# Attention and feed-forward on one core: the half-made words of the weight conversions in an idle PSUM bank

## The chip, the cores and the metric

The kernel runs on one core of one Trainium2 chip. Its time is the device time of one execution in microseconds (us); the figure before the change is the median of three runs. The profile is one execution recorded by the hardware profiler on the same core. Engines: PE is TensorE's matmul, PEld its weight load, DVE VectorE, ACT ScalarE, POOL GpSimd, SP the engine whose queue issues the DMAs.

## The reference

Attention in which a query sees only the keys of its own hash bucket, and then a feed-forward layer on the result:

```
q, k, v: (4, 8, 768, 64)      proj: (64, 6)
bucket(x) = sum over 6 bits of 2^i * (x @ proj > 0)
scores = q @ k^T / 8,  -1e9 where bucket(q) != bucket(k)
attn = exp(scores - rowmax);  attn /= sum(attn) + 1e-9
x = (attn @ v), heads side by side: (3072, 512)
h = x @ w_in (512 x 2048)
g = h if h >= 1;  0 if h <= -1;  (h + 1)^2 / 4 between
out = g @ w_out (2048 x 512)
```

The weights come as 64-bit floats. The matmuls run on rounded 32-bit numbers (fp32r); for accuracy an operand is split into a rounded high part and the low rest, and three products are added (high by high, high by low, low by high).

## The kernel before

**Heads and units.** The 32 heads (hd) are worked one after the other, two to a pair. A head has 12 units: two halves (hf) of 384 queries by six blocks (j) of 128 keys. The loop at line 609 runs over all units g, and its order is the order on every engine; the schedule is written by hand. In each turn the program issues, in this order: the score products of unit g (`s_unit`, L371 and L372) and ACT's two exponentials (L380 rounded, L385 plain); the DVE reduction of the last maximum product (`max_red`, L314), if the turn before issued one; the subtraction that makes the low part of unit g-1 (`lo_unit`, L39, on DVE, but on POOL for j = 0 and 3); the three value products of unit g-4 (`pv_unit`, L404 to L406); in every even unit two maximum products for the head after next (`max_mm`, L310); and last the tasks that are listed for that unit (`at(g, ...)`). "Unit 9" below means the turn for unit 9 of a head.

**PSUM.** There are eight banks: four score tiles in a ring (`ps_s`), two output banks (`obank`), and a two-bank tile for the maximum products (`ps_m`, tile smax, one buffer). `obank[0]` collects the value products of the first half, in units 4 to 9 of the head, and ACT copies it out (L412) behind unit 9; it then lies idle until unit 4 of the next head. `obank[1]` collects the second half, from unit 10 to unit 3 of the next head.

**Hash and maximum.** For each pair the hash products (`bits_mm`, L210: four matmuls for each half) go into an idle output bank; ACT copies the negated low rows out (L216), DVE compares (`bits_cmp`, L221), POOL scales (`bits_scale`, L273), SP puts the result in its place. Their operands are made by POOL in units 0 to 3 (`cast_h` L152, `low_h` L39, one pair of them per unit, all queued behind `max_clamp` L342). The negated row maxima of a head are clamped, transposed on PE (`max_tr`, L349) into a PSUM bank at unit 4, and copied by ACT at unit 5 (`max_put`, L354).

**Weight conversions.** `WeightSplit.steps` turns a 64-bit block (128 x 512) into a 32-bit float by integer operations: s0 loads the raw words (`wraw`), s1 squares the high word on ACT (L69) and starts the word `wa` on DVE (L70), s2 (L74) and s3 (L78) put in sign and low bits, s4 (L82) multiplies by a flag into `wsq`, s5 and s6 make the high and low parts (ACT L87, POOL L39), `put` stores. Heads 3 to 26 each begin one such conversion: twelve of w_in in the odd heads, twelve that are parked in DRAM in the even ones. `conv` lists the steps by units counted from the head's first: 0 for s0, 7 for s1, 9 for s2, 13 (unit 1 of the next head) for s3, 15 for s4. The word lives in an SBUF tile with one buffer.

**Feed-forward.** Behind the attention come the two layers (`gemm1` and the product loop, L959 and L1054 for the first, L822 for the second). Eight blocks of w_out are converted there, with POOL unused.

Of the kernel before, what the change touches and what calls it, by code (L numbers as in the profile page):

```python
# [11 lines left out]
F32 = mybir.dt.float32  # L12
F32R = mybir.dt.float32r
I32 = mybir.dt.int32
# [8 lines left out]
P = 128  # L23
# [4 lines left out]
DM = H * D  # L28
# [9 lines left out]
def sub(nc, eng, out, a, b):  # L38
    eng.tensor_tensor(out=out, in0=a, in1=b, op=ALU.subtract)  # L39


class WeightSplit:
# [7 lines left out]
        nc.vector.memset(sc[:, 1:2], 29)  # L50
        self.sc = sc

    def steps(self, src, shape, hi, lo, cp, stage=None, low=None, keep=None):
        nc, n = self.nc, self.n
        st = {}

        def s0():
            st["raw"] = self.pool.tile([P, n, 2], I32, name="wraw")
            dst = st["raw"]
            if len(shape) == 4:  # L60
                dst = dst.rearrange("p (c f) t -> p c f t", c=shape[1])
            nc.sync.dma_start(out=dst, in_=src)

        def s1():
            raw = st["raw"]
            sq = st["sq"] = self.pool.tile([P, n], F32, name="wsq")
            a = st["a"] = self.pool.tile([P, n], I32, name="wa", bufs=1)
            high = raw[:, :, 1].bitcast(F32)
            nc.scalar.activation(out=sq, in_=high, func=AF.Square)  # L69
            nc.vector.tensor_scalar(out=a, in0=raw[:, :, 1], scalar1=0x07FFFFFF, scalar2=3,  # L70
                                    op0=ALU.bitwise_and, op1=ALU.logical_shift_left)

        def s2():
            nc.vector.scalar_tensor_tensor(out=st["a"], in0=st["raw"][:, :, 1], scalar=self.sc[:, 0:1],  # L74
                                           in1=st["a"], op0=ALU.bitwise_and, op1=ALU.bitwise_or)

        def s3():
            nc.vector.scalar_tensor_tensor(out=st["a"], in0=st["raw"][:, :, 0], scalar=self.sc[:, 1:2],  # L78
                                           in1=st["a"], op0=ALU.logical_shift_right, op1=ALU.bitwise_or)

        def s4():
            nc.vector.scalar_tensor_tensor(out=st["sq"], in0=st["sq"], scalar=WMIN2,  # L82
                                           in1=st["a"].bitcast(F32), op0=ALU.is_ge, op1=ALU.mult)

        def s5():
            if cp is nc.scalar:
                cp.copy(out=hi, in_=st["sq"])  # L87
            else:
                cp.tensor_copy(out=hi, in_=st["sq"])

        def s6():
            sub(nc, low or nc.gpsimd, lo, st["sq"], hi.bitcast(F32))

        def put():
            nc.sync.dma_start(out=keep if stage is None else stage, in_=st["sq"])

        if stage is None:
            return [s0, s1, s2, s3, s4, s5, s6] + ([put] if keep is not None else [])

        def get(sq=None):  # L100
            st["sq"] = self.pool.tile([P, n], F32, name="wsq") if sq is None else sq
            nc.sync.dma_start(out=st["sq"], in_=stage)

        return [s0, s1, s2, s3, s4, put], [get, s5, s6]


# [4 lines left out]
NU = 2 * NJ  # L111


def attention(ctx, tc, wst, T1, T2, qk, v, pj, cv, x_d, s_d, e_d, tasks, shared):
    nc = tc.nc
    const = ctx.enter_context(tc.tile_pool(name="aconst", bufs=1))
    work = ctx.enter_context(tc.tile_pool(name="awork", bufs=2))
    small = ctx.enter_context(tc.tile_pool(name="asmall", bufs=2))
    shared["work"], shared["small"] = work, small
    ps_s = ctx.enter_context(tc.tile_pool(name="ps_s", bufs=4, space=PSUM))  # L120
    ps_o = ctx.enter_context(tc.tile_pool(name="ps_o", bufs=1, space=PSUM))
    ps_m = ctx.enter_context(tc.tile_pool(name="ps_m", bufs=1, space=PSUM))
    obank = [ps_o.tile([P, 512], F32, name=f"o{i}") for i in range(2)]
# [193 lines left out]
    mx = {}  # L317
# [26 lines left out]
        eng.tensor_scalar(out=nm[:, 0:NJ], in0=nm[:, 0:NJ], scalar1=CLAMP, scalar2=None,  # L344
                          op0=ALU.min)

    def max_tr(hd, bank):
        ps = mx[hd] = obank[bank]
        nc.tensor.transpose(out=ps[0:2 * NJ, 0:P], in_=nms.pop(hd), identity=ident)  # L349

    def max_put(hd):
# [98 lines left out]
    def raw0():  # L450
        return wst.tile([P, DM, 2], I32, name="wraw").rearrange("p a b -> p (a b)").bitcast(F32)[:, 0:S].rearrange(
            "p (h s) -> p h s", h=1)

    def at(g, fn, *a):
        tasks[g].append((fn, a))

    first = [raw0(), raw0()]
# [92 lines left out]
    at(12, bits_put, 1)  # L550
    at(12, move, 1, 2)
    at(12, max_tr, 0, 0)
    at(12, max_put, 0)
    at(10, load_raw, 2)
# [4 lines left out]
    at(15, row_flags, 1)  # L559
    at(12, lambda: nc.gpsimd.memset(T2[2][0:64, 0].bitcast(F32), 0.0))  # L560
    at(17, max_tr, 1, 1)
    at(17, max_put, 1)
    at(18, half_clamp, 2, 0)
# [4 lines left out]
    for hd in range(NH):  # L568
        pr, h = hd // 2, hd % 2
        g = hd * NU  # L570
        if 0 < hd < NH - 2:
            gc, gt = ((g + NU + 6, g + NU + 7) if hd == 1 else (g + NU + 2, g + NU + 4) if hd == 2
                      else (g + NU, g + NU + 4))
            at(gc, max_clamp, hd + 2, nc.gpsimd if hd > 2 else nc.vector)
            at(gt, max_tr, hd + 2, 1)
            at(gt + (hd > 1), max_put, hd + 2)
        if h == 0 and pr + 2 < NPAIR:
            g0 = g + (13, 2)[pr] if pr < 2 else g
            for n in range(4):
                at(g0 + n, cast_h, pr + 2, nc.gpsimd, n % 2, n // 2)  # L580
                at(g0 + n, low_h, pr + 2, nc.gpsimd, n % 2, n // 2)
            at(g0 + 3, move, pr + 2, 0)
            at(g0 + 3, move, pr + 2, 1)
            at(g0 + 6, move, pr + 2, 2)
            if pr + 3 < NPAIR:
                at(g0 + 7, load_raw, pr + 3)
            bits_at = ((20, 1), (23, 0)) if pr == 0 else ((8 if pr == 1 else 7, 1), (11, 0))
            for hf, (n, bank) in enumerate(bits_at):
                at(g + n, bits_mm, pr + 2, hf, bank)
                at(g + n + 1, bits_cmp, pr + 2, hf)  # L590
            at(g + n + 1, move, pr + 2, 3)
            at(g + n + (2 if pr else 1), bits_scale, pr + 2, nc.gpsimd if pr else nc.scalar)
            at(g + (18 if pr else 25), bits_put, pr + 2)
        if h == 0 and pr + 1 < NPAIR:
            gv = g + LAG + (2 if pr else 16)
            at(gv, cast_v, pr + 1, nc.scalar)
            at(gv + 1, split_v, pr + 1, nc.gpsimd, 0)
            at(gv + 3, split_v, pr + 1, nc.gpsimd, 1)
            if pr + 2 < NPAIR:
                at(gv + (6 if pr else 4), load_v, pr + 2)  # L600
# [8 lines left out]
    for g in range(NG + LAG + 1):  # L609
# [7 lines left out]
        if g < 4 * NU:  # L617
            due = g in early
            hd, i = early.get(g, (0, 0))
        else:  # L620
            hd, i = g // NU + 2, g % NU // 2
# [18 lines left out]
NCT = DM // P  # L640
# [458 lines left out]
def lsh_attn_ffn(ctx: ExitStack, tc: tile.TileContext, qk, v, pj, cv, w_in, w_out, out):  # L1099
    nc = tc.nc  # L1100
# [13 lines left out]
    wq = [xdp.tile([P, DM], F32, name=f"wq{i}") for i in range(NFT)]  # L1114
# [16 lines left out]
    wih, wil = ([w[:, t] for w in wpair] for t in range(2))  # L1131
# [3 lines left out]
    win_v = w_in.bitcast(I32).rearrange("(ct p) (f t) -> p ct f t", p=P, t=2)  # L1135
    wout_v = w_out.bitcast(I32).rearrange("(ft p) (n t) -> ft p n t", p=P, t=2)
    wst = ctx.enter_context(tc.tile_pool(name="wst", bufs=2))
    ws = WeightSplit(nc, wst, DM)
# [4 lines left out]
    def at(g, fn, *a):  # L1143
        tasks[g].append((fn, a))

    def conv(g, steps, offs):
        for fn, n in zip(steps, offs):
            at(g + n, fn)

    def wi_steps(i, cp, stage=None):  # L1150
        return ws.steps(win_v[:, :, i * P:(i + 1) * P, :], (P, NCT, P, 2), wih[i], wil[i], cp, stage, None, wq[i])

    def wo_steps(i, cp, stage=None, low=None):
        return ws.steps(wout_v[i], (P, DM, 2), woh[i], wol[i], cp, stage, low)

    woh = [hi for hi, lo in wo]
    wol = [lo for hi, lo in wo]
    for i in range(NW1):
        conv((2 * i + 3) * NU, wi_steps(i, nc.scalar), (0, 7, 9, 13, 15, 17, 19, 21))
    g0 = (NH - 4) * NU  # L1160
    late = {}
    for n in range(NSTG):
        i = n - (NFT - NW1)
        stage = wq[NW1 + n] if i < 0 else xdp.tile([P, DM], F32, name=f"wd{n}")
        if i < 0:
            first, late[n] = wi_steps(NW1 + n, nc.vector, stage)
        elif i < 2:
            first, late[n] = wo_steps(i, nc.vector, stage)
        else:
            first, late[n] = wo_steps(i, nc.scalar, stage, nc.gpsimd if i < 4 else nc.vector)  # L1170
        conv((4 + 2 * n) * NU, first, (0, 7, 9, 13, 15, 16))
    for n, g in enumerate((1, 7, 13, 25, 30, 35)):
        conv(g0 + g, late[n], (0, 5, 6))

    actx = ExitStack()
    attn = {}
    for b in range(B - 1):
        g = (b + 1) * H * NU + LAG + 4
        at(g, lambda b=b: xm.sums_load(*(attn["small"].tile([P, NF], F32, name=n, bufs=1) for n in ("sm", "em")), b))
# [21 lines left out]
    for i in (2, 3):  # L1201
        at(NH * NU + 2 * i - 10, late[i + NFT - NW1][0])
    attention(actx, tc, wst, T1, T2, qk, v, pj, cv, x_d, s_d, e_d, tasks, attn)
    actx.close()

# [5 lines left out]
    for i in range(2, NFT):  # L1211
        n = i + NFT - NW1
        need = i + GLAG if i < LEAD else 2 * i + GLAG + 1 - LEAD
        if n < NSTG:
            get, cast, low = late[n]
# [68 lines left out]
```

## Time and profile before

| | |
|---|---|
| time, median of three runs | 981.41 us (980.84 to 982.14) |
| span of the profiled execution, first to last instruction | 980.2 us |
| PE busy in the span | 966.7 us |
| DVE busy | 793.9 us |
| ACT busy | 679.6 us |
| POOL busy | 346.3 us |
| attention | up to about 463.6 us |
| granted TensorE clock | 1.000 |

The profiled execution's own time is known as its span; the runs' times stand 1.2 us above it (981.41 against 980.2), for what lies around the first and last instruction. A profile line of the timeline has the start, the length, the engine, the line of the code, the operation and the tiles (out<-in). A line of instruction groups has the count behind an x, the busy time, the mean length in ns, and then the idle time of that engine just before them. A line of waits has who waited for whom, the total in us, how often, and the longest. The lines by stretches have the length, then busy time and count of PE, PEld, DVE, ACT and POOL, the granted clock, the DMA share and GB/s.

### The profile page before, as it was taken

Reading aid. Unit: us, or ns where it says so; the run is one execution under the profiler, and the core shown is the slowest. Engines: PE = TensorE matmul, PEld = TensorE weight load, DVE = VectorE, ACT = ScalarE, POOL = GpSimd, SP = SyncE. Lnnn points to the kernel's source line nnn. Section 1 sums busy time; section 2 is a strip of 40 time slices with the busy share of each in tenths; the row PEclk is TensorE's granted clock in tenths of the full one; section 3 lists DMA queues with packets and bytes.
Section 4 is the critical chain, followed back from the end, with each engine's and each line's share of the span. In section 5 each row is a group of like instructions: output and inputs, shape, how many; then the busy total and the mean of one; then the engine's idle time right before and its main releaser. Section 6 shows DMA issues by size and latency. Waiting matters only on the chain.

```text
span 980.2 us, 15590 instructions
## 1 busy us (share of the span) xinstructions
PE 966.7 (99%) x5050; PEld 889.7 (91%) x5050; DVE 793.9 (81%) x1359; ACT 679.6 (69%) x1481; POOL 346.3 (35%) x418
## 2 busy tenths in 40 slices
PE   8999999999999999999999999999999999999998
PEld 7889999999999999999999998888988889988886
DVE  8779999999999999887898887877866777655554
ACT  7878988898899898888655555455564545544444
POOL 8767777778887777666000000000000000000000
PEclk9999999999999999999999999999999999999999
DMA  6674667676666667644395478966458554454431
GB/s 164 178 189 108 165 175 184 192 180 192 168 159 162 177 174 187 161 119 126 126 319 185 129 237 287 314 223 205 116 157 240 149 183 119 143 159 119 117 88 65
DMA packets 95113, 167.56 MB, mean 171 GB/s; under 512 B 13956, under 2 KB 51960, under 8 KB 95032
## 3 DMA queue, kind: packets, MB, share of 16 engines
q1 hardware_dynamic: 94808, 166.56, 59.6%
q8 instruction: 40, 0.66, 0.3%
q14 instruction: 41, 0.34, 0.1%
q10 hardware_dynamic: 224, 0.00, 0.0%
HBM read 106.13 MB, written 33.87 MB: 143 GB/s over the span
## 4 chain that ended last, share of the span: by engine, by line
PE 87%; DVE 5%; ACT 3%; DMA 2%; issue 1%; POOL 1%; SPq 1%; DVEq 0%; ACTq 0%; POOLq 0%
PE y L822 27%; PE h L1054 18%; PE smax L310 7%; PE h L959 7%; PE o L406 5%; PE o L404 5%; PE o L405 5%; PE s L371 5%; PE s L372 5%; DVE nm L314 2%; PE o L210 2%; DVE pl L39 1%; DMA wraw<-in_w_in_dram 1%; ACT ph L380 1%; DMA sm<-sd 0%
## 5 line engine op out<-in xcount | busy, mean ns | idle before, releaser
L380 ACT ACTIVATE ph<-s 128x384 fp32r<-128x384 f32 x380 | 188.3, 496 | 41.1 <-PE s L372 35.1
L314 DVE TENSOR_REDUCE nm<-smax 128x1 f32<-128x768 f32 x189 | 179.0, 947 | 15.2 <-PE smax L310 13.6
L39 POOL TENSOR_TENSOR pl<-pf,ph 128x384 fp32r<-128x384 f32 x128 | 141.9, 1112 | 87.8 <-ACT pf L385 83.1
L787 DVE SCALAR_TENSOR_TENSOR t<-t 128x384 f32<-128x384 f32 x128 | 71.3, 557 | 101.6 <-ACT z L782 101.3
L39 DVE TENSOR_TENSOR pl<-s,ph 128x384 fp32r<-128x384 f32 x256 | 135.8, 544 | 10.8 <-ACT s L385 9.6
L371 PE MATMUL s<-t 128*128 128x384 f32 x384 | 132.2, 344 | 0.0
L404 PE MATMUL o<-ph,va 128*128 128x386 f32 x384 | 130.1, 339 | 1.1 <-DVE neg L221 1.1
L406 PE MATMUL o<-pl,va 128*128 128x386 f32 x384 | 130.1, 339 | 0.4 <-DVE pl L39 0.4
L405 PE MATMUL o<-ph,vb 128*128 128x386 f32 x384 | 130.1, 339 | 0.0
L372 PE MATMUL s<-t 128*128 128x384 f32 x384 | 129.3, 337 | 0.0
L385 ACT ACTIVATE s<-s 128x384 f32<-128x384 f32 x252 | 125.2, 497 | 0.0
L822 PE MATMUL y<-t,ghi 128*128 128x512 f32 x384 | 124.7, 395 | 0.0
L310 PE MATMUL smax<-t 128*128 128x384 f32 x378 | 103.1, 354 | 5.7 <-DVE nm L314 4.4
L781 ACT ACTIVATE t<-h,mh 128x384 f32<-128x384 f32 x56 | 32.6, 581 | 84.0 <-PE h L959 44.3
L310 PEld LDWEIGHTS smax<-t 128*128 128x128 f32 x378 | 64.4, 188 | 23.8 <-DVE nm L314 22.1
L792 ACT CAST ghi<-z 128x384 fp32r<-128x384 f32 x129 | 65.1, 505 | 30.1 <-DVE z L788 26.3
L782 ACT ACTIVATE z<-t,m 128x384 f32<-128x384 f32 x128 | 79.0, 617 | 4.2
L1054 PE MATMUL h<-wbig,t 128*128 128x384 f32 x399 | 81.4, 336 | 0.0
L822 PEld LDWEIGHTS y<-t,ghi 128*128 128x128 f32 x384 | 71.3, 188 | 11.1 <-ACT ghi L792 0.3
L1054 PEld LDWEIGHTS h<-wbig,t 128*128 128x128 f32 x399 | 71.6, 188 | 5.3
L781 ACT ACTIVATE t<-wsq,mh 128x384 f32<-128x384 f32 x48 | 29.6, 617 | 67.0 <-DVE wsq L1067 40.8
L822 PE MATMUL y<-t,glo 128*128 128x512 f32 x192 | 76.0, 396 | 0.0
(189 smaller groups left out, 2134.9 us busy)
## 6 DMA issues: line engine op xcount, KB each, us to landing
t<-wc SPq DMA_DIRECT2D x92, 256.0 KB
t<-t SPq DMA_DIRECT2D x60, 384.0 KB
wraw<-wc SPq DMA_DIRECT2D x76, 256.0 KB
raw<-in_qk_dram SPq DMA_DIRECT2D x14, 768.0 KB
wraw<-in_w_in_dram SPq DMA_DIRECT2D x16, 512.0 KB
wraw<-in_w_out_dram SPq DMA_DIRECT2D x16, 512.0 KB
t<-ed SPq DMA_DIRECT2D x36, 192.0 KB
xd<-xs SPq DMA_DIRECT2D x32, 192.5 KB
```

Of the source, the lines that this page charges most:

```text
L39: eng.tensor_tensor(out=out, in0=a, in1=b, op=ALU.subtract)
L310: nc.tensor.matmul(out=smax[hd][:, hf, 0:HS], lhsT=t2[:, 0, h, i * P:(i + 1) * P], rhs=t2[:, 1, h, hf * HS:(hf + 1) * HS], start=True, sto ...
L314: nc.vector.tensor_reduce(out=nmp(hd)[:, i:i + 1], in_=smax[hd][:, :, 0:HS], axis=AX.XY, op=ALU.max, negate=True)
L371: nc.tensor.matmul(out=ps[:, 0:HS], lhsT=t1[:, 1, h, ks], rhs=t1[:, 0, h, sl], start=True, stop=False)
L372: nc.tensor.matmul(out=ps[:, 0:HS], lhsT=t2[:, 1, h, ks], rhs=t2[:, 0, h, sl], start=False, stop=True)
L380: nc.scalar.activation(out=ph[:, 0:HS], in_=ps[:, 0:HS], func=AF.Exp, scale=SCALE)
L385: nc.scalar.activation(out=pf, in_=ps[:, 0:HS], func=AF.Exp, scale=SCALE)
L404: nc.tensor.matmul(out=o, lhsT=wa, rhs=ph, start=(jj == 0), stop=False)
L405: nc.tensor.matmul(out=o, lhsT=wb, rhs=ph, start=False, stop=False)
L406: nc.tensor.matmul(out=o, lhsT=wa, rhs=pl, start=False, stop=(jj == NJ - 1))
L822: nc.tensor.matmul(out=ys[c][m], lhsT=g_[:, m * P:(m + 1) * P], rhs=w, start=(first and k == 0), stop=(last and k == 2))
L1054: nc.tensor.matmul(out=ps, lhsT=w[:, cs], rhs=x, start=(n == 0 and s not in (2, 3, 6)), stop=(n == 5), skip_group_check=True)
```

## The change

The word of the conversions moves from SBUF into `obank[0]`, for the 24 conversions in the attention (those in the feed-forward part keep the SBUF tile). As that bank is idle only from unit 10 to unit 3 of the next head, the steps move: s1 and s2 both to unit 10, s3 to 12 (unit 0 of the next head), s4 to 14 (unit 2), s5, s6 and `put` one unit earlier. The hash products of a pair, from the fourth pair on, go one after the other into `obank[1]`, at units 5 and 7 in place of 7 (bank 1) and 11 (bank 0); the comparison, SP's last move and POOL's scale step follow them, at units 6 and 8, 8, and 9. The transposed maxima, which had lain in `obank[1]` at unit 4, take a tile of the score ring, from the sixth head's maxima on.

```diff
-    def steps(self, src, shape, hi, lo, cp, stage=None, low=None, keep=None):
+    def steps(self, src, shape, hi, lo, cp, stage=None, low=None, keep=None, word=None):
...
-            a = st["a"] = self.pool.tile([P, n], I32, name="wa", bufs=1)
+            a = st["a"] = self.pool.tile([P, n], I32, name="wa", bufs=1) if word is None else word()
...
-    shared["work"], shared["small"] = work, small
+    shared["work"], shared["small"], shared["word"] = work, small, lambda: obank[0].bitcast(I32)
...
-    def max_tr(hd, bank):
-        ps = mx[hd] = obank[bank]
+    def max_tr(hd, bank=None):
+        ps = mx[hd] = ps_s.tile([P, 512], F32, name="s") if bank is None else obank[bank]
...
-            at(gt, max_tr, hd + 2, 1)
+            at(gt, max_tr, hd + 2, 1 if hd < 3 else None)
...
-            bits_at = ((20, 1), (23, 0)) if pr == 0 else ((8 if pr == 1 else 7, 1), (11, 0))
+            bits_at = (((20, 1), (23, 0)), ((8, 1), (11, 0)))[pr] if pr < 2 else ((5, 1), (7, 1))
...
-        return ws.steps(win_v[:, :, i * P:(i + 1) * P, :], (P, NCT, P, 2), wih[i], wil[i], cp, stage, None, wq[i])
+        return ws.steps(win_v[:, :, i * P:(i + 1) * P, :], (P, NCT, P, 2), wih[i], wil[i], cp, stage, None, wq[i], word)
...
-        return ws.steps(wout_v[i], (P, DM, 2), woh[i], wol[i], cp, stage, low)
+        return ws.steps(wout_v[i], (P, DM, 2), woh[i], wol[i], cp, stage, low, None, None if stage is None else word)
...
-        conv((2 * i + 3) * NU, wi_steps(i, nc.scalar), (0, 7, 9, 13, 15, 17, 19, 21))
+        conv((2 * i + 3) * NU, wi_steps(i, nc.scalar), (0, 10, 10, 12, 14, 16, 18, 20))
...
-        conv((4 + 2 * n) * NU, first, (0, 7, 9, 13, 15, 16))
+        conv((4 + 2 * n) * NU, first, (0, 10, 10, 12, 14, 15))
```

More of the change, by code (lines that the diff above doesn't have):

```diff
@@ L1148, in conv, with word @@
             at(g + n, fn)
+    attn = {}
+    def word():
+        return attn["word"]()
     def wi_steps(i, cp, stage=None):
-        return ws.steps(win_v[:, :, i * P:(i + 1) * P, :], (P, NCT, P, 2), wih[i], wil[i], cp, stage, None, wq[i])
+        return ws.steps(win_v[:, :, i * P:(i + 1) * P, :], (P, NCT, P, 2), wih[i], wil[i], cp, stage, None, wq[i], word)
     def wo_steps(i, cp, stage=None, low=None):
-        return ws.steps(wout_v[i], (P, DM, 2), woh[i], wol[i], cp, stage, low)
+        return ws.steps(wout_v[i], (P, DM, 2), woh[i], wol[i], cp, stage, low, None, None if stage is None else word)
     woh = [hi for hi, lo in wo]
@@ L1175, in lsh_attn_ffn @@
     actx = ExitStack()
-    attn = {}
     for b in range(B - 1):
```

## The prediction

> **What bounds the kernel now.** I read the page's first part, then busy time by stretches, then the waits of the stretch that holds the edits, then single heads in the timelines.
>
> ```profile
> span 980.2 us, 15590 instructions
> PE 966.7 (99%) x5050; PEld 889.7 (91%) x5050; DVE 793.9 (81%) x1359; ACT 679.6 (69%) x1481; POOL 346.3 (35%) x418
> ...
> PE 87%; DVE 5%; ACT 3%; DMA 2%; issue 1%; POOL 1%; SPq 1%; DVEq 0%; ACTq 0%; POOLq 0%
> ```
>
> PE has work nearly all the time and makes 87% of the chain that ended last. The edits take no matmul away, so they can only win or lose what PE waits. Head 4 begins at 79.8 us and head 28 at 412.9; the feed-forward part begins at about 463.6.
>
> ```profile
> 79.80:412.90 333.10, 332.24 (x1850) 318.19 (x1849) 315.15 (x465) 300.38 (x720) 255.60 (x288) 1.00 0.65 172
> ...
> 463.60:980.20 516.60, 512.38 (x2546) 459.59 (x2544) 371.32 (x718) 273.93 (x517) 2.55 (x2) 1.00 0.57 175
> ```
>
> The columns after the length are PE, PEld, DVE, ACT and POOL. In those 24 heads DVE is busy 315.15 of 333.10 us, 95%. Busy PE hides short waits, because a matmul's record covers its pipeline, so I count starts instead.
>
> ```profile
> 271.75 0.33 PE L371 MATMUL s<-t 128*128 128x384 f32 x1
> ...
> 272.62 0.33 PE L371 MATMUL s<-t 128*128 128x384 f32 x1
> ...
> 273.85 0.33 PE L371 MATMUL s<-t 128*128 128x384 f32 x1
> ...
> 275.60 0.52 PE L310 MATMUL smax<-t 128*128 128x384 f32 x2
> 275.96 0.33 PE L371 MATMUL s<-t 128*128 128x384 f32 x1
> ```
>
> These are the starts of units 9, 10 and 11 of head 17 and of unit 1 of head 18. From 271.75 to 275.96 there are 24 matmuls and no wait: 4.21/24 = 0.1754 us each. A pair of heads has 24 units of five matmuls, 24 maximum products (L310) and 8 hash products (L210), 152 in all: 26.66 us.
>
> ```profile
> 252.24 0.51 PE L310 MATMUL smax<-t 128*128 128x384 f32 x2
> ...
> 252.87 0.34 PE L372 MATMUL s<-t 128*128 128x384 f32 x1
> ```
>
> L372 would come three starts after 252.24, at 252.77, and comes at 252.87: a transpose costs 0.10 us, two per pair, 26.86 us in all. A pair took 333.10/12 = 27.76. So PE waits 0.90 us per pair, 0.45 per head, 10.8 us in the stretch. The waits there name one cause:
>
> ```profile
> PEld smax L310 <- DVE nm L314: 11.9, 40, 0.4
> ...
> DVE wa L70 <- DMA wraw<-in_w_in_dram: 3.4, 7, 1.0
> ```
>
> A maximum product waits for the DVE reduction of the one before it (one smax tile). What counts is when each reduction ends, not DVE's mean load.
>
> **How such a wait arises**, to test the method on what is known:
>
> ```profile
> 244.06 0.96 DVE L314 TENSOR_REDUCE nm<-smax 128x1 f32<-128x768 f32 x1 [0.21 <-PE smax L310]
> 244.94 0.55 DVE L39 TENSOR_TENSOR pl<-s,ph 128x384 fp32r<-128x384 f32 x1
> 245.40 1.58 DVE L74 SCALAR_TENSOR_TENSOR wa<-wraw,wsc,wa 128x512 int32<-128x512 int32 x1
> 246.91 0.94 DVE L314 TENSOR_REDUCE nm<-smax 128x1 f32<-128x768 f32 x1
> ```
>
> ```profile
> 246.84 0.34 PE L371 MATMUL s<-t 128*128 128x384 f32 x1
> ...
> 247.91 0.62 PE L310 MATMUL smax<-t 128*128 128x384 f32 x2
> 248.37 0.35 PE L371 MATMUL s<-t 128*128 128x384 f32 x1
> ```
>
> The 1.58 us word step delays the reduction to 247.85. Head 16 begins at 246.84; its first maximum product, due five matmuls later at 247.72, starts at 247.91, and unit 1 at 248.37: 0.52 us after the reduction's end. Successive DVE instructions start 0.07 to 0.08 us before the last one's recorded end (244.06 + 0.96 against 244.94). I use these two numbers below.
>
> **The word operations.** The same four instructions, first in the stretch, then in the feed-forward part, where POOL works 2.55 us in all:
>
> ```profile
> L314 DVE TENSOR_REDUCE nm<-smax 128x1 f32<-128x768 f32 x145 | 137.0, 945 | 4.2 <-PE smax L310 2.8
> L39 DVE TENSOR_TENSOR pl<-s,ph 128x384 fp32r<-128x384 f32 x192 | 101.1, 542 | 4.5 <-ACT s L385 4.5
> L78 DVE SCALAR_TENSOR_TENSOR wa<-wraw,wsc,wa 128x512 int32<-128x512 int32 x24 | 27.2, 1135 | 0.0
> L82 DVE SCALAR_TENSOR_TENSOR wsq<-wsq,wa 128x512 f32<-128x512 f32 x24 | 25.7, 1071 | 0.0
> L74 DVE SCALAR_TENSOR_TENSOR wa<-wraw,wsc,wa 128x512 int32<-128x512 int32 x24 | 25.2, 1050 | 0.0
> L221 DVE TENSOR_TENSOR neg<-o,neg 32x384 f32<-32x384 f32 x24 | 13.0, 540 | 5.7 <-ACT neg L216 5.7
> L70 DVE TENSOR_SCALAR wa<-wraw 128x512 int32<-128x512 int32 x23 | 12.6, 547 | 3.4 <-DMA wraw<-in_w_in_dram 3.4
> ```
>
> ```profile
> L74 DVE SCALAR_TENSOR_TENSOR wa<-wraw,wsc,wa 128x512 int32<-128x512 int32 x8 | 6.0, 752 | 0.3
> L78 DVE SCALAR_TENSOR_TENSOR wa<-wraw,wsc,wa 128x512 int32<-128x512 int32 x8 | 6.0, 745 | 0.0
> L82 DVE SCALAR_TENSOR_TENSOR wsq<-wsq,wa 128x512 f32<-128x512 f32 x8 | 5.5, 692 | 0.4
> L70 DVE TENSOR_SCALAR wa<-wraw 128x512 int32<-128x512 int32 x8 | 3.4, 419 | 0.0
> L809 DVE COPY pcs<-y 128x512 f32<-128x512 f32 x1 | 0.7, 691 | 3.4 <-PE y L822 3.4
> ```
>
> Beside a busy POOL the three with two SBUF inputs take 1.05 to 1.14 us, alone 0.69 to 0.75. The subtraction pl<-s,ph, with one input in PSUM, holds 0.54 beside the same POOL. With the word in PSUM I charge L74, L78 and L82 their lone times. L70 then writes to PSUM; no row shows that. Its ends are 0.42 (the lone row, SBUF to SBUF) and 0.69 (L809, the same 128x512 with PSUM on one side). I take 0.69, since L809 has the bank in its path. The Trainium skill (VectorE: DVE Perf Modes, section on Mode 2×_2P) says that the mode that doubles a one-input instruction's rate needs source and destination in SBUF; it speaks against this edit, and by it the sum is the one below, while with the short form kept it is that of rival B. DVE's load falls by 90.7 - 24 x (0.69 + 0.75 + 0.745 + 0.69) = 21.7 us; that alone saves no PE time.
>
> **The steps in other units.** Before, L70 ran at unit 7, L74 at 9, L78 at unit 1 of the next head, L82 at 3. After: L70 and L74 both at 10, L78 at 0, L82 at 2. In DVE's order unit 10 had nothing; now both sit ahead of the reduction of unit 10's product. And L70 must wait until ACT has copied bank 0 out (L412), which ACT does after unit 9's two exponentials:
>
> ```profile
> 272.38 0.50 ACT L380 ACTIVATE ph<-s 128x384 fp32r<-128x384 f32 x1
> ...
> 273.12 0.51 ACT L412 COPY xs<-o 128x384 f32<-128x384 f32 x1
> ```
>
> Unit 9 began at 271.75, so the copy ends 1.88 us after it; with the Square (L69) moved behind it perhaps 1.85. The chain, counted from unit 9's start: copy 1.85; L70 1.90, L74 2.52, reduction 3.19 to 4.14. The next head's first product is due at 3.86 and unit 1 at 4.21; it comes at 4.14 + 0.52 = 4.66, a loss of 0.45. DVE goes on: the subtractions of units 10 and 11 at 4.06 and 4.53, L78 at 5.00, the reduction of unit 0 from 5.67 to 6.62. Unit 3 starts at 6.62 + 0.52 = 7.13. Undisturbed it is 36 matmuls after unit 9: 36 x 0.1754 = 6.31. Loss 0.82 us per head. Then one subtraction (0.47), L82 (0.62) and the reduction (0.95) make 2.03 us against the 2.1 that PE takes for two units: no third loss. L82 ends near 7.7, before unit 4 needs bank 0 at 8.36, so the new wait of L404 on L82 costs nothing (0.65 us cover).
>
> A pair after: 26.86 + 2 x 0.82 = 28.50 against 27.76, +0.74, times 12 pairs: +8.9 us. All 24 boundaries, from head 3's end to head 26's, fall in the stretch. Waits before came from the old places of the word steps, so they are gone in this count. The seven waits of L70 for the raw weights (3.4 us of DVE) go too: the transfer gets three units more.
>
> **The hash products**, from units 7 and 11 (banks 1 and 0) to 5 and 7 (both bank 1): the same eight matmuls, 1.4 us. They leave unit 11, where they gave DVE 0.7 us more before the next head's first product; that is why both heads of a pair now lose alike. The second set waits until the first is compared: set 1 ends 1.75 after unit 5's start, ACT's copy (0.5, an estimate from L412's 0.51) by 2.3, DVE's comparison (L221, 0.54) by 2.9, and set 2 is due at 3.68 (units 5 and 6, 0.88 + 0.70 + 1.23, and 0.88): nothing lost, 0.8 us cover. Without it, half a microsecond late would be 6 us over 12 heads. Set 2 also needs POOL's fourth subtraction:
>
> ```profile
> 247.94 0.23 POOL L342 TENSOR_SCALAR nm<-nm 128x6 f32<-128x6 f32 x1 [1.51 <-DVE nm L314]
> ...
> 251.41 0.51 POOL L152 CAST t<-raw 128x384 fp32r<-128x384 f32 x1
> ...
> 252.95 0.97 POOL L152 CAST t<-raw 128x384 fp32r<-128x384 f32 x1
> ...
> 255.55 1.02 POOL L39 TENSOR_TENSOR t<-raw,t 128x384 fp32r<-128x384 f32 x1
> ```
>
> In head 16, from 246.84, it ends at +9.73; due is unit 7's end, seven units 7.54, transpose 0.10, set 1 0.70, losses 0.82, own five 0.88: 10.04. The clamp, behind the late reduction, starts 0.15 later: 9.88, and POOL gets back 0.46 where the cast of 0.97 takes 0.51 again. Cover 0.16 to 0.62; should POOL be one blocked cast (0.46) later than that, 0.3 would be missed in 12 heads, 3.6 us, which I keep for the range. Their scale step runs on POOL four units earlier, ahead of the subtraction of unit 9, which PE needs at the next head's unit 3, over 1 us later than POOL has it. SP's last move of the pair comes at unit 8 in place of 12, behind the same queue: hidden by the rest of the head.
>
> **The transposes** go to the ring of four score tiles. Unit 5's scores then wait for unit 2's subtraction, not unit 1's. It follows the reduction that lets unit 4's product go by 0.47 us, and that product plus the transpose take 0.52 before unit 5: nothing, 0.05 us cover; without it up to 0.05 x 24 = 1 us. The last steps on ACT, POOL and SP come one unit earlier: each ends well ahead of its next use.
>
> **Sum.** 980.2 + 8.9 = 989.1 for the profiled span; 1.2 us lies around it, so against the median 981.41: 990.3 us.
>
> **Rivals.** B: L70 keeps 0.42. The chain is 0.27 shorter, loss 0.55, pair 27.96, +2.4 us: 983.8. For it: 419 ns in eight cases; against: the only row with PSUM on a side. C, faster: word instructions on the bank cost so little that the chain fits. At 0.42 for each of L70, L74 and L78 it is 6.20, under 6.31, and all waits go: 981.4 - 10.8 = 970.6. It decides at a chain of 6.76, the present loss of 0.45, 0.37 us shorter than mine over the three. For it: the lock with POOL goes; against: L74 and L78 need 0.75 with POOL idle. D: POOL still blocks L74 and L78, 1.58 in place of 0.75 once per head: +0.83 x 24 = 20, 1010 us; pl<-s,ph at 0.54 is against it.
>
> **Chances.** My case 0.62, B 0.14, C 0.19, D 0.05. Two runs of this kernel can tell about 0.2%, 2 us. C is faster (0.19); half of B is within 2 us (0.07); the rest slower (0.74). The range reaches down into C to 979 and up over POOL's 3.6 us and 2 us of unknown size to 996.
>
> **What would show it.** L70 near 0.69 and L74, L78, L82 near 0.7 with little spread; L70 starting at L412's end; the first units of every head from 4 to 27 late by 0.45 and 0.38; heads near 13.6 and 14.9 us; no PE wait at units 6 and 10. Wrong, if the reduction of unit 10 ends less than 3.8 us after unit 9's start.

## The result, and the profile after

The changed kernel takes 992.39 us (median; 991.91 to 994.66), the kernel before on the same chip 981.77: ratio 1.0108, 95% interval 1.0094 to 1.0123. It is slower by 10.6 us, where 8.9 were forecast.

The page's first part and the head of the chain that ended last:

```profile
span 990.5 us, 15604 instructions
PE 970.2 (98%) x5050; PEld 889.6 (90%) x5050; DVE 780.8 (79%) x1359; ACT 678.6 (69%) x1481; POOL 317.2 (32%) x418
...
PE 73%; DVE 13%; ACT 5%; DMA 3%; issue 3%; POOL 2%; SPq 0%; POOLq 0%; DVEq 0%; ACTq 0%
```

DVE and POOL both work less than before (780.8 against 793.9 us, 317.2 against 346.3), and yet DVE's share of the chain rises from 5% to 13%. The stretch from head 4's start to head 28's, and the feed-forward part:

```profile
79.90:423.40 343.50, 335.60 (x1850) 318.15 (x1849) 302.29 (x465) 299.96 (x721) 226.63 (x288) 1.00 0.62 167
474.30:990.50 516.20, 512.32 (x2546) 459.51 (x2544) 371.48 (x718) 273.89 (x517) 2.55 (x2) 1.00 0.58 175
```

With the same 1850 matmuls the first takes 343.50 in place of 333.10 us: the whole loss. The feed-forward part keeps its length (516.2 against 516.6). In that stretch, the waits and DVE's groups:

```profile
PEld smax L310 <- DVE nm L314: 23.3, 48, 0.7
```

```profile
L74 DVE SCALAR_TENSOR_TENSOR o<-wraw,wsc,o 128x512 int32<-128x512 int32 x24 | 18.1, 755 | 0.8
L78 DVE SCALAR_TENSOR_TENSOR o<-wraw,wsc,o 128x512 int32<-128x512 int32 x24 | 17.9, 746 | 0.0
L82 DVE SCALAR_TENSOR_TENSOR wsq<-wsq,o 128x512 f32<-128x512 f32 x24 | 16.3, 677 | 0.0
L70 DVE TENSOR_SCALAR o<-wraw 128x512 int32<-128x512 int32 x23 | 16.0, 696 | 4.7 <-ACT xs L412 4.7
```

The bank does what it can do: L74, L78 and L82 fall from 1050, 1135 and 1071 ns to their lone times, L70 grows from 547 to 696. The word steps cost DVE 68 us in place of 91. PE's wait for the reductions doubles all the same, from 11.9 to 23.3 us. One boundary shows how; first DVE, then PE, in the timeline of head 16's end and head 17's start:

```profile
264.59 0.55 DVE L39 TENSOR_TENSOR pl<-s,ph 128x384 fp32r<-128x384 f32 x1
265.34 0.69 DVE L70 TENSOR_SCALAR o<-wraw 128x512 int32<-128x512 int32 x1 [0.20 <-ACT xs L412]
266.07 0.76 DVE L74 SCALAR_TENSOR_TENSOR o<-wraw,wsc,o 128x512 int32<-128x512 int32 x1
266.73 0.95 DVE L314 TENSOR_REDUCE nm<-smax 128x1 f32<-128x768 f32 x1
267.60 1.01 DVE L39 TENSOR_TENSOR pl<-s,ph 128x384 fp32r<-128x384 f32 x2
268.53 0.75 DVE L78 SCALAR_TENSOR_TENSOR o<-wraw,wsc,o 128x512 int32<-128x512 int32 x1
269.18 0.95 DVE L314 TENSOR_REDUCE nm<-smax 128x1 f32<-128x768 f32 x1
```

```profile
263.52 0.33 PE L371 MATMUL s<-t 128*128 128x384 f32 x1
...
266.50 0.33 PE L371 MATMUL s<-t 128*128 128x384 f32 x1
...
267.74 0.62 PE L310 MATMUL smax<-t 128*128 128x384 f32 x2 [0.20 <-DVE nm L314]
268.20 0.35 PE L371 MATMUL s<-t 128*128 128x384 f32 x1
...
269.09 0.34 PE L371 MATMUL s<-t 128*128 128x384 f32 x1
...
270.19 0.62 PE L310 MATMUL smax<-t 128*128 128x384 f32 x2
270.65 0.34 PE L371 MATMUL s<-t 128*128 128x384 f32 x1
```

Unit 9 starts at 263.52. L70 waits for ACT's copy and starts 1.82 later, unit 1 of the next head comes at 4.68 in place of 4.21, unit 3 at 7.13 in place of 6.31. The starts of L371 show the same at all 24 boundaries. From one head's start to the next, odd heads take 13.56 us and even heads 14.97 (medians), against 13.05 and 14.8 before; only heads 10, 18 and 26 take longer, 15.3 us.

### The profile page after: what moved, and what is told of

It is laid out like the page before. It is cut to its first block, busy times and chain, and to the rows that moved or that the text cites. A ratio compares the mean times of both kernels' runs of the same rounds, so it can differ in the third digit from the quotient of the medians.

```text
span 990.5 us, 15604 instructions
## 1 busy us (share of the span) xinstructions
PE 970.2 (98%) x5050; PEld 889.6 (90%) x5050; DVE 780.8 (79%) x1359; ACT 678.6 (69%) x1481; POOL 317.2 (32%) x418
## 4 chain that ended last, share of the span: by engine, by line
PE 73%; DVE 13%; ACT 5%; DMA 3%; issue 3%; POOL 2%; SPq 0%; POOLq 0%; DVEq 0%; ACTq 0%
PE y L822 26%; PE h L1054 18%; PE h L959 7%; DVE nm L314 5%; PE smax L310 5%; PE s L371 3%; PE s L372 3%; PE o L406 3%; PE o L404 3%; PE o L405 3%; DVE pl L39 3%; DMA t<-t 2%; DVE o L78 1%; PE o L210 1%; DVE o L70 1%
## 5 line engine op out<-in xcount | busy, mean ns | idle before, releaser
L314 DVE TENSOR_REDUCE nm<-smax 128x1 f32<-128x768 f32 x189 | 180.4, 955 | 28.3 <-PE smax L310 26.9
L39 POOL TENSOR_TENSOR pl<-pf,ph 128x384 fp32r<-128x384 f32 x128 | 130.4, 1019 | 116.3 <-ACT pf L385 112.0
L39 DVE TENSOR_TENSOR pl<-s,ph 128x384 fp32r<-128x384 f32 x256 | 138.3, 550 | 23.9 <-ACT s L385 15.4
L371 PE MATMUL s<-t 128*128 128x384 f32 x384 | 132.3, 344 | 0.2 <-DVE pl L39 0.2
L310 PE MATMUL smax<-t 128*128 128x384 f32 x378 | 103.7, 355 | 12.6 <-DVE nm L314 10.6
L822 PE MATMUL y<-woh,glo 128*128 128x512 f32 x192 | 75.7, 394 | 0.2
```

Source lines behind the costliest of these rows:

```text
L310: nc.tensor.matmul(out=smax[hd][:, hf, 0:HS], lhsT=t2[:, 0, h, i * P:(i + 1) * P], rhs=t2[:, 1, h, hf * HS:(hf + 1) * HS], start=True, sto ...
L314: nc.vector.tensor_reduce(out=nmp(hd)[:, i:i + 1], in_=smax[hd][:, :, 0:HS], axis=AX.XY, op=ALU.max, negate=True)
L371: nc.tensor.matmul(out=ps[:, 0:HS], lhsT=t1[:, 1, h, ks], rhs=t1[:, 0, h, sl], start=True, stop=False)
L822: nc.tensor.matmul(out=ys[c][m], lhsT=g_[:, m * P:(m + 1) * P], rhs=w, start=(first and k == 0), stop=(last and k == 2))
```

## The experiments

Edits are against the changed kernel, but where another is named. Ratios are to the kernel before on the same chip. Loss per head means PE's wait at the boundary, read from the starts of its matmuls. In the changed kernel it has two parts: unit 1 comes 4.69 us after unit 9 in place of 4.21 (0.48), and unit 3 falls back further, by 0.34 at most boundaries and 0.39 on the mean.

**The word back in SBUF, steps where the change put them.**

```diff
-    ... wih[i], wil[i], cp, stage, None, wq[i], word)
+    ... wih[i], wil[i], cp, stage, None, wq[i])
-    ... cp, stage, low, None, None if stage is None else word)
+    ... cp, stage, low)
```

> The changed kernel with the word back in its SBUF tile, and nothing else undone: the steps stay at units 10, 10, 0 and 2. My theory (the order of DVE's work between unit 9 and unit 3 of the next head sets the loss): L70 no longer waits for the copy and is short again, so the reduction of unit 10 ends near 3.5 us after unit 9's start and the first loss goes; but the word steps block with POOL again. At lone times the loss per head is 0.2, at the mean times before the change (1.05 to 1.14 us) about 0.9: 24 times that less the 0.45 of before, so 976 to 992 us, most likely 988. Rival (the PSUM bank itself costs the time, by the slow form of L70 and the wait for the copy): back to the kernel before, 982 us or less.

999.94 us, ratio 1.0185 (1.0170 to 1.0201): outside what I gave, on the side away from the rival. The bank is no cause of the loss; at these places it saves 7.5 us. I had taken mean lengths; what counts is what POOL is doing when each instruction starts. At unit 10 of an odd head POOL has just begun a subtraction (timelines of DVE and POOL of this run):

```profile
282.60 1.26 DVE L70 TENSOR_SCALAR wa<-wraw 128x512 int32<-128x512 int32 x1
```

```profile
282.56 1.02 POOL L39 TENSOR_TENSOR pl<-pf,ph 128x384 fp32r<-128x384 f32 x1 [2.28 <-ACT pf L385]
```

L70 starts 0.04 us behind POOL and takes 1.26 us, three times its lone 0.42. In even heads it is L74 that meets POOL: 1.38 us in place of 0.75. So the chain is longer with the short form of L70 and no copy to wait for than with the bank: unit 3 of an even head comes 7.47 us after unit 9, of an odd head 7.21, against 7.13.

**Hash products and transposes alone.** The word in SBUF and its steps at the old units; only units 5 and 7 in bank 1 and the ring tile remain of the change. (The first lines of the edit are those of the run above.)

```diff
...
-        conv((2 * i + 3) * NU, wi_steps(i, nc.scalar), (0, 10, 10, 12, 14, 16, 18, 20))
+        conv((2 * i + 3) * NU, wi_steps(i, nc.scalar), (0, 7, 9, 13, 15, 17, 19, 21))
...
-        conv((4 + 2 * n) * NU, first, (0, 10, 10, 12, 14, 15))
+        conv((4 + 2 * n) * NU, first, (0, 7, 9, 13, 15, 16))
```

> The kernel before with only the hash products moved to units 5 and 7 and the transposes moved into the score ring; the word stays in SBUF and its steps at units 7, 9, 1 and 3. My theory: neither costs anything by itself, and the reduction of unit 10 ends 0.3 us ahead of need even without the 0.7 us of hash products at unit 11: 982 us, within 2. Rival (the lost slack at unit 11 and the POOL deadline of the second set make the loss in the even heads): half of the 10.6 us and more, 987 us or above.

982.3 us, ratio 1.0003 (0.9994 to 1.0013): no cost as a whole. Its parts moved, though. DVE now waits for the raw weights longer than the 3.4 us of before:

```profile
DVE wa L70 <- DMA wraw<-in_w_in_dram: 14.1, 11, 1.9
```

Even heads got about 0.3 us shorter and some odd ones up to 1 us longer, and the two cancel. Why the weights land later I did not test, so what the move costs or saves without that wait stays open.

**L74 to unit 11, L78 to unit 1.**

```diff
-        conv((2 * i + 3) * NU, wi_steps(i, nc.scalar), (0, 10, 10, 12, 14, 16, 18, 20))
+        conv((2 * i + 3) * NU, wi_steps(i, nc.scalar), (0, 10, 11, 13, 14, 16, 18, 20))
-        conv((4 + 2 * n) * NU, first, (0, 10, 10, 12, 14, 15))
+        conv((4 + 2 * n) * NU, first, (0, 10, 11, 13, 14, 15))
```

> The changed kernel with L74 at unit 11 in place of 10 and L78 at unit 1 of the next head in place of 0, the word still in the bank. My theory, by the same chain: unit 10's reduction starts behind L70 alone, at 2.46 us from unit 9's start, so the first product is on time; unit 3 is 0.1 late; the reduction of unit 2 comes behind L78 and L82 and costs 0.5. Loss 0.60 per head in place of 0.87: 24 x 0.27 = 6 us less than the changed kernel, 986 us. Rival (the bank or the hash products cost the time): 992 us as it was.

986.65 us, ratio 1.0047 (1.0031 to 1.0064), as expected: the same instructions in the same bank, 5.7 us less for two numbers in a list. That the size fits is partly luck. Most heads gain 0.32 us on the changed kernel, more than the 0.27 expected, and heads 10, 18 and 26 take 0.44 longer. There a small sum of an image (L667) now meets POOL and takes 0.96 us; in the changed kernel it takes 0.19:

```profile
L667 DVE TENSOR_SCALAR sm<-sm 128x48 f32<-128x48 f32 x3 | 2.9, 958 | 0.1
```

**Each of the two moves alone.** First L74:

```diff
-        conv((2 * i + 3) * NU, wi_steps(i, nc.scalar), (0, 10, 10, 12, 14, 16, 18, 20))
+        conv((2 * i + 3) * NU, wi_steps(i, nc.scalar), (0, 10, 11, 12, 14, 16, 18, 20))
...
+        conv((4 + 2 * n) * NU, first, (0, 10, 11, 12, 14, 15))
```

> The changed kernel with L74 alone moved, from unit 10 to 11; L78 stays at unit 0. My theory counts the whole chain to unit 3: the first product comes on time, but L74 then stands in front of the reduction of unit 0 together with two subtractions and L78, which ends at 6.55 and lets unit 3 go at 7.07, loss 0.76 per head in place of 0.87: 24 x 0.11 = 3 us less, 989.5 us. Rival (the two losses are separate, 0.48 and 0.39, and this takes the first away): 24 x 0.48 = 11.5 us less, 981 us.

991.03 us, ratio 1.0092 (1.0075 to 1.0109). The wait at unit 0 is gone, and unit 2 has nearly all of it: unit 1 starts 4.21 us after unit 9, unit 3 at 7.00. DVE's timeline at one boundary: unit 10's reduction comes right behind L70, but L74 now stands in the way of unit 0's reduction, the second L314:

```profile
263.62 0.69 DVE L70 TENSOR_SCALAR o<-wraw 128x512 int32<-128x512 int32 x1 [0.20 <-ACT xs L412]
264.22 0.95 DVE L314 TENSOR_REDUCE nm<-smax 128x1 f32<-128x768 f32 x1
265.08 0.55 DVE L39 TENSOR_TENSOR pl<-s,ph 128x384 fp32r<-128x384 f32 x1
265.55 0.75 DVE L74 SCALAR_TENSOR_TENSOR o<-wraw,wsc,o 128x512 int32<-128x512 int32 x1
266.20 0.55 DVE L39 TENSOR_TENSOR pl<-s,ph 128x384 fp32r<-128x384 f32 x1
266.67 0.75 DVE L78 SCALAR_TENSOR_TENSOR o<-wraw,wsc,o 128x512 int32<-128x512 int32 x1
267.33 0.95 DVE L314 TENSOR_REDUCE nm<-smax 128x1 f32<-128x768 f32 x1
```

Then L78:

```diff
+        conv((2 * i + 3) * NU, wi_steps(i, nc.scalar), (0, 10, 10, 13, 14, 16, 18, 20))
...
+        conv((4 + 2 * n) * NU, first, (0, 10, 10, 13, 14, 15))
```

> The changed kernel with L78 alone moved, from unit 0 to unit 1 of the next head; L70 and L74 both stay at unit 10. My theory: the first loss of 0.48 stays, the second (0.39) goes, because the reduction of unit 0 no longer follows L78; L78 and L82 then delay the reduction of unit 2 by 0.2. Loss 0.68 in place of 0.87, 24 x 0.19 = 4.5 us less: 988 us. Rival (separate losses): 24 x 0.39 = 9 us less, 983 us.

987.67 us, ratio 1.0056 (1.0041 to 1.0071). Both come near the sum over the whole chain (989.5 and 988), and far from separate losses (981 and 983). Unit 1 stays at 4.69 and unit 3 comes at 6.80, so the second loss is gone; 0.15 of it comes back by unit 5, where 0.2 was expected.

**The subtraction of unit 11 on POOL.** The steps stay where the change put them.

```diff
-        return g % NJ in POOL_J
+        return g % NJ in POOL_J or g % NU == NU - 1 and 3 * NU <= g < 27 * NU
```

> The changed kernel with the subtraction of unit 11 on POOL in place of DVE in heads 3 to 26; the steps stay where the change put them. My theory: 0.47 us leaves DVE's chain between the two reductions, so the second loss goes (unit 3 late by 0.4 in place of 0.87), 24 x 0.47 = 11 us less: 981 us; POOL's casts start 0.7 later in the even heads, cover 1.08 us at the second set of hash products, so that costs 0 to 2 us. Rival (the wait of L70 for the copy alone, or the bank): 0 to 1 us less, 991 us.

985.65 us, ratio 1.0039 (1.0024 to 1.0054): 6.7 us less where I expected 11. The way was right and the size not: 0.47 us leaves the chain, but the second loss was only 0.39, and the wait at unit 0 cannot shrink, since this instruction stands behind it. That makes 24 x 0.39 = 9.4 us. Most odd heads give a part back: their unit 5 comes 9.07 us after unit 9, that of the even heads mostly 8.93. ACT's plain exponential waits there until POOL has freed one of the two `pf` tiles, and DVE's work behind it is late. The waits from 79.8 to 420 us of this run have

```profile
ACT pf L385 <- POOL pl L39: 8.8, 12, 0.9
```

About 0.60 per head remains.

**Both edits at once.**

```diff
+        return g % NJ in POOL_J or g % NU == NU - 1 and 3 * NU <= g < 27 * NU
...
+        conv((2 * i + 3) * NU, wi_steps(i, nc.scalar), (0, 10, 11, 13, 14, 16, 18, 20))
...
+        conv((4 + 2 * n) * NU, first, (0, 10, 11, 13, 14, 15))
```

> Both last edits at once: L74 at unit 11, L78 at unit 1, and the subtraction of unit 11 on POOL in heads 3 to 26; the word in the bank. My theory: DVE's chain then fits, the reduction of unit 2 is late by 0.1 in place of 0.5, loss about 0.16 per head: 986.6 - 24 x 0.43 = 976 us. But POOL's casts start about 1.5 us later at the head of an even head, behind that subtraction and a clamp that would otherwise be done at 1.0, and their last one meets the second set of hash products (due near 9.2): 0 to 0.5 lost in 12 heads, so 976 to 982 us, most likely 979. Rival (the bank or the hash products cost the time): 986 us or more.

984.88 us, ratio 1.0025 (1.0016 to 1.0035), above my range. The reductions hardly hold PE any more; POOL does, and not where I looked. The waits from 79.8 to 415 us of this run:

```profile
PEld o L406 <- POOL pl L39: 7.4, 11, 1.0
PEld smax L310 <- DVE nm L314: 4.7, 18, 0.4
```

I had expected POOL to be late for the hash products of the even heads. It was late at the end of them, for the low part of unit 11 that it had just been given; PE needs that at unit 2 of the odd head.

**Both edits, unit 10 in the odd heads.** There POOL can start before the next head's clamp. The sums of an image, which stood in the chain of heads 10, 18 and 26, also go elsewhere. The steps stand as in the run above.

```diff
-        return g % NJ in POOL_J
+        return g % NJ in POOL_J or g % NU == NU - 1 - g // NU % 2 and 3 * NU <= g < 27 * NU
...
-        at(g + 15, xm.sums_add)
-        at(g + 21, xm.sums_inv, b)
+        at(g + 23, xm.sums_add)
+        at(g + 25, xm.sums_inv, b)
```

> As the run with both edits, but in the odd heads it is the subtraction of unit 10 that goes to POOL (its exponentials are done before the next head's clamp, so the casts keep their time), in the even heads that of unit 11; and the three small sums of each image go to quiet units of the following head (15 and 21 become 23 and 25). My theory: no lateness at the hash products, loss about 0.16 per head, and the three heads that lost 1.1 us more to the sums lose nothing: 973 to 976 us, faster than both kernels. Rival (POOL or the bank sets a floor): 979 us or more.

975.57 us, ratio 0.9927 (0.9913 to 0.9942): faster than both kernels. The sums, however, gained nothing. L666 and L667, in the groups of this run and then in those of the next:

```profile
L666 DVE SCALAR_TENSOR_TENSOR sm<-em,sm 128x48 f32<-128x48 f32 x3 | 3.6, 1189 | 0.0
L667 DVE TENSOR_SCALAR sm<-sm 128x48 f32<-128x48 f32 x3 | 2.8, 918 | 0.1
```

```profile
L666 DVE SCALAR_TENSOR_TENSOR sm<-em,sm 128x48 f32<-128x48 f32 x3 | 1.0, 343 | 0.9 <-DMA sm<-sd 0.9
L667 DVE TENSOR_SCALAR sm<-sm 128x48 f32<-128x48 f32 x3 | 0.6, 189 | 0.1
```

48 columns took 1.19 us next to a busy POOL. The next run, otherwise as this one, puts them into the odd head:

```diff
+        at(g + 10, xm.sums_add)
+        at(g + 12, xm.sums_inv, b)
```

> The faster version of before (both edits, mixed POOL units) with the small sums of an image at units 6 and 8 of the odd head instead of units 7 and 9 of the even one. My theory: in the even head, where POOL is busy, the two sums took 1.17 and 0.93 us for 48 elements against 0.20 and 0.19 elsewhere, the same block by POOL as the word steps had, and three pairs of heads lost 1.1 us each; in the odd head POOL is mostly idle, so 3 x 1.1 = 3.3 us less: 972 us. Rival (the place among DVE's own work costs, not POOL): 975.5 us as it was.

972.39 us, ratio 0.9901 (0.9886 to 0.9915), the best of all: 9.5 us less than the kernel before on the same chip. The wait of PE's weight loads for the reductions, from 78 to 420 us of this run:

```profile
PEld smax L310 <- DVE nm L314: 1.1, 2, 0.9
```

In the heads of the stretch unit 1 now starts 4.21 us after unit 9 and unit 3 at 6.31 (both within 0.03), the figures of a PE without waits: now that less stands ahead of the reductions that PE needs, the loss at the boundaries is gone, with the word still in the bank.

**The same relief without the bank.** The edit is against the kernel before:

```diff
-        return g % NJ in POOL_J
+        return g % NJ in POOL_J or g % NU == NU - 1 and 3 * NU <= g < 27 * NU
```

> The kernel before with only the subtraction of unit 11 moved to POOL in heads 3 to 26: is the bank needed for a gain, or is it the load taken off DVE alone? My theory: the loss at unit 0 (0.2 in every second head) goes, but POOL, at 77% here and blocked by the word steps, gets late for the hash products at unit 7 and for the values, which takes about as much: 980 us, 977 to 986. Rival (DVE's load is all that counts, whatever the place of the word): 24 x 0.47 = 11 us less, 971 us.

994.0 us, ratio 1.0116 (1.0101 to 1.0131): outside what I gave, on the side away from the rival. Taking load off DVE makes this kernel slower, because the word steps in SBUF block with the POOL that got it. L82, in the groups of heads 4 to 27 of this run:

```profile
L82 DVE SCALAR_TENSOR_TENSOR wsq<-wsq,wa 128x512 f32<-128x512 f32 x24 | 38.7, 1614 | 0.0
```

It took 1071 ns before and 677 with the bank. So the rival that DVE's load alone counts (971 us) falls, and this relief needs the bank at these places. It is not shown that no schedule with the word in SBUF gains: the choice of unit 10 or 11 by head and the moved sums were run only with the bank.

## Why the prediction was right

**The chain.** It said, from unit 9's start: L70 1.90, L74 2.52, reduction 3.19 to 4.14, unit 1 at 4.66, unit 3 at 7.13. Measured at head 16's end: 1.82, 2.55, 3.21 to 4.16, 4.68, 7.13. Two small errors cancel, which is luck: with the Square behind it the copy ends at 1.79, not 1.85, but L74 starts 0.04 after L70's end in place of 0.07 before it.

```profile
264.82 0.49 ACT L412 COPY xs<-o 128x384 f32<-128x384 f32 x1
```

The two lone moves and the spread version confirm that the chain as a whole counts, within 1.6 us.

**L70's form.** 0.696 us, as taken from the one row with PSUM on a side; rival B (0.42 kept) falls. The Trainium skill (VectorE: DVE Perf Modes, What auto-detection actually checks) makes it a condition of the mode with two results per cycle for one source (2×_2P) that source and destination are both in SBUF. The 0.696 against 0.419 agrees. Rival D falls too: L74, L78 and L82 take 755, 746 and 677 ns, each within 4 ns, beside a POOL that works 226.63 of 343.50 us. The Trainium skill (SBUF — State Buffer, Who interferes with whom) says that a DVE instruction with at most one SBUF input, outside the modes that use two ports, does not contend with GpSimd. The rows of L70, L74, L78 and L82 agree, if their tensors are counted (`wsc` in L74 and L78 is one value for each partition). Rival C needed the chain at 6.76 or less, and it was 7.13.

**Hash products, transposes, POOL.** No cost as a whole, as the run with them alone shows. POOL's fourth subtraction ended 8.98 us into head 16 (from 251.50), 1.1 ahead of its use (PE's L210 at 261.57), more than the 0.16 to 0.62 of cover that I gave. POOL's timeline, before and then after:

```profile
250.00 1.47 POOL L39 TENSOR_TENSOR pl<-pf,ph 128x384 fp32r<-128x384 f32 x1
```

```profile
254.85 1.00 POOL L39 TENSOR_TENSOR pl<-pf,ph 128x384 fp32r<-128x384 f32 x1
...
257.34 0.51 POOL L152 CAST t<-raw 128x384 fp32r<-128x384 f32 x1
...
259.47 1.02 POOL L39 TENSOR_TENSOR t<-raw,t 128x384 fp32r<-128x384 f32 x1
```

I had counted on one instruction becoming short again, the cast of 0.97 us; the subtraction of 1.47 us did so too. Of these 0.94 us the clamp, 0.19 later than before, takes a part.

**The sum.** The stretch grew by 10.4 us, not 8.9. The term that was too small is the loss of three heads: heads 10, 18 and 26 wait 0.34 us more at unit 2, where the sums of an image stand in the same chain (unit 11 of the head before); I had left them out of it, 1.0 us. The rest, about 0.02 per head, lies outside the boundary, whose 0.82 came out as forecast: the 26.86 us of a pair without waits are a little too few.

## What to carry to other kernels

Where two engines run in step, read an in-order queue as a chain between two hand-overs and add up what stands ahead of each; an engine's total load says little (here it fell by 13 us and the kernel lost 10.6). A resource that is free only late moves work into a part of the cycle that may be full: before paying for it, look which instruction it puts ahead of the one that others wait for. If a faster form is bound to a bad place, keep the form and shift the neighbours: here two list entries, one subtraction per head and three small sums turned +10.6 us into -9.5.

## What the runs showed of the hardware that I had not expected

How much a DVE instruction loses to POOL does not follow from its own length, but from the POOL instructions that it meets. The two sums of 48 columns went from 0.20 and 0.19 us up to 1.19 and 0.92, and L70 from 0.42 to 1.26 us when POOL began 0.04 us earlier: 0.73 to 0.99 us more, next to POOL instructions of 1.0 to 1.3 us. One such instruction is not the limit. In the run with the word in SBUF and the subtraction of unit 11 on POOL, L82, 0.69 us alone, took up to 2.2 us in the odd heads and 1.0 to 1.3 in the even ones (timelines of DVE and POOL):

```profile
99.77 2.16 DVE L82 SCALAR_TENSOR_TENSOR wsq<-wsq,wa 128x512 f32<-128x512 f32 x1
```

```profile
99.43 0.97 POOL L273 TENSOR_SCALAR bits<-neg,cvt 32x768 fp32r<-32x768 f32 x1
100.38 1.00 POOL L39 TENSOR_TENSOR pl<-pf,ph 128x384 fp32r<-128x384 f32 x1
```

It lasts over the rest of one POOL instruction and the whole of the next, and ends 0.55 us behind that one; L70 above ended 0.28 us behind its one. A mean over a kernel's run hides this, because the same schedule repeats the same meetings: before the change, L74's mean of 1.05 us was 0.73 or 0.74 in 14 heads, 1.58 or 1.59 in eight, and between in two.
